# A second PSUM bank by turns for the products of the Fourier transforms

## The chip, the cores and the metric

The kernel runs on one core of a Trainium2 chip. The metric is the device time of one execution in microseconds (us). TensorE (PE, with its weight loads PEld) does the matmuls and writes PSUM; VectorE (DVE) and ScalarE (ACT) read PSUM; GpSimd (POOL) works on SBUF; SyncE (SP) issues most DMAs. All data are float32; a float32 matmul shows as two records on PE.

## The reference

```python
X = np.fft.rfft(x, axis=1)                    # x: 8 x 3008 x 256
Y = X * (filt_r + 1j * filt_i)[None, :, :]
y = np.fft.irfft(Y, n=3008, axis=1)
h = y.reshape(24064, 256) @ w_in              # 256 x 2048
g = h - np.tanh(h)
out = g @ w_out                               # 2048 x 256
```

## The kernel before

Two pieces of work lie side by side. The first is the filter in the frequency domain. A transform of 3008 points is done as 64 x 47, so each batch takes four steps of matmuls with constant matrices, with transposing trips through DRAM between them:

- `first`: 64-point transform, product `pf` (L351, L361), copied out by ACT (L352, L363).
- `middle`: 47-point transform, product `pz` (L430); then the filter: ACT writes a copy of `pz` with its halves exchanged to `zs` (L443, L444), DVE multiplies `pz` into `uv` (L445), POOL multiplies `zs` and adds it to `uv` (L446, L447). Then the inverse 47-point transform, product `pe` (L411), copied out by ACT (L414).
- `last`: inverse 64-point transform, product `pu` (L511), copied to `ut` by ACT (L513); POOL makes the sums `tu` of it (L524 to L527).

`middle` is a generator. Of its steps, one issues `pz` and what follows it, the next issues the `pe` of the step before. So `pz` and `pe` take turns, and a `pe` reads a `uv` that was begun one `pz` earlier. The second piece is the dense layer: up by `w_in` (`up`, L545), the nonlinearity (`shrink`, L611 to L621), down by `w_out` (`down`, L663). Both matrix products go by a scheme with seven block products in place of eight.

The batches are in five groups of one or two, `UNITS = [(0,), (1, 2), (3, 4), (5, 6), (7,)]`. While the dense layer of one of them runs, the transforms of the next are done in its gaps. The start ("prologue") does the transforms of batch 0 and has PSUM tiles of its own. Then a loop runs over 192 dense units `U`; four units make a quarter-by-quarter pass over the 2048 hidden columns for one chunk of rows. Unit `U` issues the `up` of `U`, the `shrink` of `U - 1` and the `down` of `U - 2`. The order on every engine is fixed by this program, since the schedule is manual.

Within `up`, `t(0)` to `t(4)` are the five places where one step of a transform is let in, at most one each. Here is the order around them on TensorE; `d()` issues matmuls of `down`:

```
X 1, Y 2, t(0), d, t(1), X 6, Z 5, d, t(2), X 7, d, t(3), X 4, d, t(4), Z 3
```

The numbers are the seven products. `X`, `Y` and `Z` are banks of PSUM. ACT copies `X` out after products 1, 6 and 7 (L551: `s1`, `u2`, `u3`), and DVE after product 4 (L590). DVE reads `Z` at L583 and L596. `Y` is written once, by product 2, and read once, by L569 on DVE. L569 is issued after `t(0)` and before `t(1)`. From there to the next unit's product 2 nothing uses `Y`.

A pool in which every tag has one buffer divides PSUM: `x`, `y`, `z`, four accumulators `o0` to `o3` of `down`, and `t`. Each is one of the eight banks. All products of the transforms in the loop are in `t`:

```python
psums.append(lambda name, shape: ps.tile(shape, F32, tag="t", bufs=1, name=name))
```

A new tile of a tag waits for the readers of the last tile of that tag. When steps of the transforms come is set by a list of positions (`steps`), and for `last` by the fourth unit of each chunk (slots 0 and 2). While batch 0's dense layer runs, in its units 8 to 21, nearly every slot has a product; later, for the pairs, less than half of the slots have one.

Of the kernel before, what the change touches and what calls it, by code (L numbers as in the profile page):

```python
# [9 lines left out]
F32 = mybir.dt.float32  # L10
# [38 lines left out]
def chunks_of(unit, size):  # L49
    n = steps_of(unit)  # L50
    return [(r, min(size, n - r)) for r in range(0, n, size)]
# [92 lines left out]
def kernel(  # L144
# [24 lines left out]
    def dram(t, off, dims):  # L169
        return bass.AP(tensor=t, offset=off, ap=[list(d) for d in dims])  # L170
# [136 lines left out]
    def weights_slow(tiles, quarters):  # L307

        jobs = parts_of(quarters)
        began = [begun(tiles, job, True) for job in jobs[:2]]  # L310
        yield
        for k in range(len(jobs)):
            for _ in began[k]:
                yield
            if k + 2 < len(jobs):
                began.append(begun(tiles, jobs[k + 2], True))
            if k % 2:
                sums(quarters[k // 2])
                yield
# [136 lines left out]
    def filter_rows(a, z):  # L456


        n, src = min(z, NK - 1) - a, (filt_r.tensor, filt_i.tensor)
        for row, m in ((0, LO), (LO, 16), (LO + 16, HI - 16)):  # L460
            low = row < LO
            at = a + 1 + NQ * row if low else NQ * (row - LO + 1) - 1 - a
            for v in range(2):
                yield v, row, m, 0, n, dram(src[v], at * DM,
                                            [[NQ * DM, m], [DM if low else -DM, n], [1, DM]])
        if z == NK:
            for v in range(2):
                yield v, v, LO - v, n, 1, dram(src[v], v * NQ * DM,
                                               [[NQ * DM, LO - v], [DM, 1], [1, DM]])
                yield v, LO, HI, n, 1, dram(src[v], NQ // 2 * DM,  # L470
                                            [[NQ * DM, HI], [DM, 1], [1, DM]])
# [282 lines left out]
    def store_some(n):  # L754
        for dst, src in outs[:n]:
            nc.sync.dma_start(dst, src)
        del outs[:n]
# [76 lines left out]
    psums = []  # L834
# [4 lines left out]
    with tc.tile_pool(name="tr", bufs=2) as tr, tc.manual_schedule():  # L839
        with tc.tile_pool(name="pro", bufs=1) as pro, \  # L840
# [136 lines left out]
            for j in range(NK // 2):  # L977
# [7 lines left out]
                for i in range(2):  # L985
                    k = (2 * j + i) % 4
# [34 lines left out]
        with tc.tile_pool(name="dn", bufs=2) as dn, \  # L1021
                tc.tile_pool(name="ps", bufs=1, space=bass.MemoryType.PSUM) as ps:

            psums.append(lambda name, shape: ps.tile(shape, F32, tag="t", bufs=1, name=name))

            y_sums = dn.tile([128, 2 * 4 * len(groups)], F32, bufs=1, name="y_sums")

            def psl(shape, tag):
                return ps.tile(shape, F32, tag=tag, bufs=1, name="pt")

            def tiles1(k, dtype, n):

                tag = {"raw": "ft", "it": "uv", "pt": "zs", "st": "e1", "ft": "a2"}[k]
                return tr.tile([128, n], dtype, tag=tag, bufs=2, name=k)

            def filters_d():
                zero = tr.tile([128, 4 * DM], F32, tag="a2", bufs=2, name="zero")
                G.memset(zero, 0.0)
                for p, bs in enumerate(UNITS[1:], 1):
                    nc.sync.dma_start(  # L1040
                        dram(ct1[p], NR * 64 * len(bs) * DM, [[DM, 64 * len(bs)], [1, DM]]),
                        zero[0:64 * len(bs), 0:DM])
                yield
                lo, hi = NR * 2 * NK * DM, IM * 2 * NK * DM
                while lo < hi:
                    n = min(128 * 4 * DM, hi - lo) // 128
                    nc.sync.dma_start(dram(filt_d, lo, [[n, 128], [1, n]]), zero[:, 0:n])
                    lo += 128 * n
                nc.sync.dma_start(dram(filt_d, (NK + NK - 1) * DM, [[DM, 1], [1, DM]]),
                                  zero[0:1, 0:DM])  # L1050
                yield
                for v, row, m, i, n, src in filter_rows(0, NK):
                    G.dma_start(dram(filt_d, ((row * 2 + v) * NK + i) * DM,
                                     [[2 * NK * DM, m], [DM, n], [1, DM]]), src)
                    yield

            late, copies = weights_slow(tiles1, range(7, 8)), filters_d()
            total = 4 * len(groups)
            for _ in last(0, z1):
                pass  # L1060
            next(late)
            for U in range(total + 2):
                i, u = divmod(U, 4)
                if U < total:
                    p, c = groups[i]
                    if c == 0 and u == 0:
                        units = 4 * len(CHUNKS[p])
                        steps, done = [], 0 if p else EARLY
                        if p + 1 < len(UNITS):
                            n_f = len(chunks_of(UNITS[p + 1], XH))  # L1070
                            n_m = 2 * NK // (3 - len(UNITS[p + 1]))
                            steps = [0.01 * units + 1.36 * units * (k - done) / (n_f - done)
                                     for k in range(n_f)]
                            lo, hi = 1.6 * units, 5 * units - 17
                            steps += [lo + (hi - lo) * k / n_m for k in range(n_m)]
                            ms = None
                    if u == 0 and i + 1 < len(groups) and c + 1 < len(CHUNKS[p]):
                        e2s[i + 1] = load_e2(*groups[i + 1])
                    if u == 2 and i + 1 < len(groups) and c + 1 == len(CHUNKS[p]):
                        assert done == len(steps)  # L1080
                        e2s[i + 1] = load_e2(*groups[i + 1])
                    if u == 0 and c + 1 == len(CHUNKS[p]) and p + 2 < len(UNITS):
                        fs = first(p + 2, z1)
                        next(fs)
                    if u == 2 and i + 1 < len(groups):
                        lasts = last(i + 1, z1)
                sh = shrink(U - 1) if 0 <= U - 1 < total else iter(())
                dw = down(U - 2) if 0 <= U - 2 < total else iter(())

                def d():  # L1090

                    next(dw, None)

                def e():

                    next(dw, None)

                def s():

                    next(sh, None)  # L1100

                def t(k):


                    nonlocal ms, done
                    if k == 2 and stores:
                        store(*stores.pop())
                    store_some(4)
                    if U >= total:
                        return  # L1110
                    pos = 20 * c + 5 * u + k
                    if u == 3 and k in (0, 2) and i + 1 < len(groups):
                        next(lasts)
                    elif done < len(steps) and steps[done] <= pos:
                        if done < n_f:
                            next(fs)
                        else:
                            next(ms)
                        done += 1
                        if done == n_f:  # L1120
                            ms = middle(p + 1, z1)
                            next(ms)
                    next(late, None)
                    if U > 0 and k in (1, 3):
                        next(copies, None)

                if U < total:
                    if U == total - 1:
                        one = tr.tile([128, 128], F32, tag="x", bufs=3, name="one_sb")
                        nc.sync.dma_start(one, one_d)  # L1130
                        ones = cst.tile([128, 1], F32, name="ones")
                        G.memset(ones, 1.0)
                    up(U, d, e, s, t)
                else:
                    for k in range(5):
                        s()
                        s()
                        d()
                        e()
                        t(k)  # L1140
                        if U == total + 1 and k == 0:
                            bounded(z1)
            for w in stores:
                store(*w)
            store_some(len(outs))
# [36 lines left out]
```

## Time and profile before

| | |
|---|---|
| time | 2831.02 us, median of 3 runs (2830.42 to 2831.22) |
| profiled span | 2831.1 us, granted TensorE clock 0.99 |
| busy, share of the span | PE 96%, PEld 80%, DVE 68%, ACT 66%, POOL 63% |
| chain that ended last | PE 78%, ACT 9%, issue 5%, DVE 5%, DMA 2% |

TensorE is busy in nearly every slice after the first two of forty. Ends of matmuls are modelled in the profile, so a short stall can hide within a busy time; starts are measured. A line of the timeline gives start, duration, engine, source line, operation, tiles, shapes and, in brackets, the idle time of the engine before it and what ended it. A line of the waits gives who waited for what: us in total, times, longest.

### The profile page before, as it was taken

Reading aid. Unit: us, or ns where it says so; the run is one execution under the profiler, and the core shown is the slowest. Engines: PE = TensorE matmul, PEld = TensorE weight load, DVE = VectorE, ACT = ScalarE, POOL = GpSimd, SP = SyncE. Lnnn points to the kernel's source line nnn. Section 1 sums busy time; section 2 is a strip of 40 time slices with the busy share of each in tenths; the row PEclk is TensorE's granted clock in tenths of the full one; section 3 lists DMA queues with packets and bytes.
Section 4 is the critical chain, followed back from the end, with each engine's and each line's share of the span. In section 5 each row is a group of like instructions: output and inputs, shape, how many; then the busy total and the mean of one; then the engine's idle time right before and its main releaser. Section 6 shows DMA issues by size and latency. Waiting matters only on the chain.

```text
span 2831.1 us, 36652 instructions
## 1 busy us (share of the span) xinstructions
PE 2730.9 (96%) x12438; PEld 2269.8 (80%) x12438; DVE 1911.7 (68%) x2175; ACT 1878.5 (66%) x2790; POOL 1792.0 (63%) x1407
## 2 busy tenths in 40 slices
PE   4899999999999999999999999999999999999998
PEld 2577777988878777888877887788888888898887
DVE  6755556666766677666666777676676767677776
ACT  2466666666666677666677666666666676667665
POOL 5546777544777767644576777755466667655555
PEclk7999999999999999999999999999999999999999
DMA  9854443233233322222333223212222322101010
GB/s 249 217 179 118 104 116 76 71 94 85 59 81 85 77 67 54 57 81 81 85 81 74 70 66 86 49 40 68 58 65 62 79 56 53 34 18 26 16 22 17
DMA packets 322592, 217.53 MB, mean 77 GB/s; under 512 B 224782, under 2 KB 274746, under 8 KB 322156
## 3 DMA queue, kind: packets, MB, share of 16 engines
q1 hardware_dynamic: 266826, 157.28, 23.6%
q10 hardware_dynamic: 52818, 51.53, 6.0%
q0 software_dynamic: 2752, 6.30, 0.8%
q8 instruction: 100, 1.64, 0.2%
q14 instruction: 96, 0.79, 0.1%
HBM read 138.87 MB, written 79.17 MB: 77 GB/s over the span
## 4 chain that ended last, share of the span: by engine, by line
PE 78%; ACT 9%; issue 5%; DVE 5%; DMA 2%; POOL 1%; ACTq 1%; SPq 0%; DVEq 0%; POOLq 0%
PE o L663 31%; PE x L545 20%; PE z L545 9%; PE y L545 6%; PE pe L411 3%; PE pu L511 3%; ACT y L611 3%; PE pz L430 3%; PE pf L351 2%; DVE h L617 1%; ACT u L551 1%; ACT zs L444 1%; DVE uv L445 1%; ACT y L612 1%; ACT zs L443 1%
## 5 line engine op out<-in xcount | busy, mean ns | idle before, releaser
L663 PE MATMUL o<-t,wd 128*128 128x256 f32 (+2 forms) x3072 | 776.3, 375 | 1.8 <-POOL t L526 1.3
L617 DVE TENSOR_TENSOR h<-h,y 128x1024 f32<-128x1024 f32 (+2 forms) x384 | 571.3, 1488 | 275.8 <-ACT y L612 275.8
L663 PEld LDWEIGHTS o<-t,wd 128*128 128x128 f32 x3072 | 580.7, 190 | 74.2 <-POOL t L526 1.6
L545 PE MATMUL x<-tu,wu 128*128 128x256 f32 (+2 forms) x2304 | 588.0, 377 | 9.2 <-ACT u L551 9.0
L663 PE MATMUL o<-h,wd 128*128 128x256 f32 (+2 forms) x2304 | 582.5, 375 | 0.4 <-DVE h L621 0.4
L621 DVE SCALAR_TENSOR_TENSOR h<-sq,h 128x1024 f32<-128x1024 f32 (+2 forms) x384 | 568.0, 1479 | 20.6 <-ACT y L611 0.5
L524 POOL TENSOR_TENSOR t<-h 128x512 f32<-128x512 f32 (+2 forms) x192 | 240.4, 1252 | 506.8 <-DVE h L621 455.0
L545 PEld LDWEIGHTS x<-tu,wu 128*128 128x128 f32 x2304 | 427.4, 190 | 151.8 <-issue 72.6
L663 PEld LDWEIGHTS o<-h,wd 128*128 128x128 f32 x2304 | 431.1, 190 | 71.8 <-issue 18.4
L618 ACT ACTIVATE sq<-y,near_b 128x1024 f32<-128x1024 f32 (+2 forms) x384 | 435.6, 1134 | 5.0 <-DVE h L621 0.2
L611 ACT ACTIVATE y<-h 128x1024 f32<-128x1024 f32 (+2 forms) x384 | 400.0, 1042 | 15.7 <-ACT e L414 8.0
L612 ACT ACTIVATE y<-y 128x1024 f32<-128x1024 f32 (+2 forms) x384 | 399.2, 1040 | 12.2
L551 ACT COPY s<-x 128x512 f32<-128x512 f32 (+2 forms) x192 | 110.8, 577 | 441.0 <-PE x L545 432.4
L527 POOL TENSOR_TENSOR t<-t,h 128x512 f32<-128x512 f32 (+2 forms) x192 | 308.9, 1609 | 0.1
L551 ACT COPY u<-x 128x512 f32<-128x512 f32 (+2 forms) x384 | 219.2, 571 | 56.9 <-PE x L545 22.2
L583 DVE TENSOR_TENSOR h<-z,u 128x512 f32<-128x512 f32 (+2 forms) x192 | 129.5, 675 | 180.0 <-ACT u L551 177.0
L525 POOL TENSOR_TENSOR t<-h,t 128x512 f32<-128x512 f32 (+2 forms) x192 | 240.9, 1255 | 15.1
L526 POOL TENSOR_TENSOR t<-h 128x512 f32<-128x512 f32 (+2 forms) x191 | 248.0, 1298 | 0.0
L446 POOL TENSOR_TENSOR zs<-zs,ft 128x512 f32<-128x512 f32 x112 | 165.4, 1477 | 101.8 <-ACT zs L444 101.6
L447 POOL TENSOR_TENSOR uv<-uv,zs 128x512 f32<-128x512 f32 x112 | 213.7, 1908 | 15.7 <-DVE uv L445 7.2
L545 PE MATMUL x<-ut,wu 128*128 128x256 f32 (+2 forms) x768 | 199.2, 382 | 6.9 <-DVE h L590 5.2
L569 DVE TENSOR_TENSOR h<-y,s 128x512 f32<-128x512 f32 (+2 forms) x192 | 130.4, 679 | 104.9 <-PE y L545 88.6
(122 smaller groups left out, 3380.2 us busy)
## 6 DMA issues: line engine op xcount, KB each, us to landing
a<-ct SPq DMA_DIRECT2D x64, 384.0 KB, 4.1
ft<-filt SPq DMA_DIRECT2D x96, 256.0 KB, 4.6
out_dram<-ot SPq DMA_DIRECT2D x1392, 16.0 KB, 1.5
ct<-e ACTq DMA_DIRECT2D x112, 192.0 KB, 2.4
ct<-a ACTq DMA_DIRECT2D x80, 256.0 KB, 2.9
x_sb<-in_x_dram SPq DMA_DIRECT2D x69, 256.0 KB, 2.8
e<-ct SPq DMA_DIRECT2D x33, 512.0 KB, 4.7
fg<-fg SPq DMA_DIRECT2D x40, 392.0 KB, 6.0
```

Source lines behind the costliest of these rows:

```text
L524: G.tensor_sub(t[0], b[0][1], b[0][0])
L525: G.tensor_sub(t[1], b[1][1], t[0])
L526: (V if shared else G).tensor_sub(t[2], b[1][1], b[0][1])
L527: G.tensor_sub(t[3], t[1], b[1][0])
L545: nc.tensor.matmul(bank[:, k], wu[:, q - 1, (2 * u + k) * 128:(2 * u + k + 1) * 128], rhs[q - 1], start=(first and k == 0), stop=True, ski ...
L551: ACT.copy(t, X)
L611: ACT.activation(y[k], ht[k], AF.Arctan, scale=S)
L612: ACT.activation(y[k], y[k], AF.Square, accum_out=y_sums[:, 2 * U + k // 2:2 * U + k // 2 + 1])
L617: V.tensor_mul(ht[k], ht[k], y[k])
L618: ACT.activation(sq[k], y[k], AF.Square, bias=near_b, scale=A)
L621: V.scalar_tensor_tensor(out=ht[k], in0=sq[k], scalar=K, in1=ht[k], op0=ALU.add, op1=ALU.mult)
L663: nc.tensor.matmul(product(q), wd[:, q - 1, (2 * u + k) * 128: (2 * u + k + 1) * 128], rhs[q - 1][:, k], start=(u == 0 and k == 0 and q == ...
```

## The change

The products of the transforms get a second bank, `Y`'s own, in those slots of a unit in which `Y` is free by the program's order: `t(1)`, `t(2)` and `t(3)`. There the tags go by turns: if the last product was in `t`, the next is in `y`, and otherwise in `t`. In `t(0)` and `t(4)` it is always `t`. The purpose is that a product need not wait until the one before it has been read.

```diff
-            psums.append(lambda name, shape: ps.tile(shape, F32, tag="t", bufs=1, name=name))
+            quarter, latest = [1], ["t"]
+
+            def zd(name, shape):
+                latest[0] = "y" if quarter[0] in (1, 2, 3) and latest[0] == "t" else "t"
+                return ps.tile(shape, F32, tag=latest[0], bufs=1, name=name)
+
+            psums.append(zd)
...
                     nonlocal ms, done
+                    quarter[0] = k
                     if k == 2 and stores:
```

The prologue keeps its own tiles. The two `pu` before the loop are at `quarter` 1: the first is in `y`, the second in `t`. In the unit with slots 0, 1, 2, 3, 4 all filled the banks are `t`, `y`, `t`, `y`, `t`. Of the 403 products from those two `pu` to the kernel's end, 164 are in `y`: 57 `pe`, 47 `pz`, 36 `pf`, 24 `pu`.

## The prediction

> **What bounds the kernel now.** I read the page first. TensorE is busy nearly always, and its idle time lies almost all in the start.
>
> ```profile
> PE 2730.9 (96%) x12438; PEld 2269.8 (80%) x12438; DVE 1911.7 (68%) x2175; ACT 1878.5 (66%) x2790; POOL 1792.0 (63%) x1407
> ```
>
> Busy time of matmuls is modelled, so I measured TensorE by the starts of its records instead. Equal records that follow each other start every 0.216 us (256 columns) or 0.433 us (512 columns). A stall is a start, less the start of the record before and that record's pace. From 150 us on, stalls sum to about 71 us, 2.5% of the span, and that bounds any gain there. Some 35 us of it stands before a product of the dense units into `x` (L545), spread thinly; 23 us before `pe` (L411), and these lie together: 22 us between 240 and 500 us. The windows show the same stage (start:end, then busy us of PE, PEld, DVE, ACT, POOL, then clock):
>
> ```profile
> 240.00:320.00 80.00, 73.41 (x295) 54.16 (x294) 45.13 (x51) 54.08 (x81) 64.44 (x46) 0.98 0.52 127
> ...
> 500.00:600.00 100.00, 100.00 (x472) 86.63 (x472) 63.50 (x74) 65.66 (x99) 46.45 (x40) 1.00 0.30 81
> ```
>
> In 240 to 320 us PE is short by 6.6 us of 80; at 500 us it is short by nothing. The first of these is where group 0's dense units (8 to 21) carry a transform product in nearly each of their five slots `t(0)` to `t(4)`; later stages fill less than half. The waits of TensorE, longest first, and one of DVE:
>
> ```profile
> PE pe L411 <- DVE uv L445: 15.3, 23, 2.7
> ```
> ```profile
> DVE uv L445 <- ACT zs L444: 124.5, 81, 5.2
> ```
>
> `pe` reads neither `pz` nor the `uv` just begun: its own `uv` is a step older. It waits for L445 because that is the last of three readers of `pz` (L443 and L444 on ACT, L445 on DVE), and `pz` holds the only bank, `t`. The timeline of unit 9 (start, us, engine, line; in brackets idle before it):
>
> ```profile
> 263.55 1.02 PE L430 MATMUL pz<-a,fg 94*128 94x512 f32 x2
> ...
> 266.58 0.59 ACT L443 ACTIVATE zs<-pz 64x512 f32<-64x512 f32 x1
> ...
> 267.18 0.58 ACT L444 COPY zs<-pz 64x512 f32<-64x512 f32 x1
> ...
> 267.44 0.59 PE L663 MATMUL o<-t,wd 128*128 128x256 f32 x2
> 267.61 1.23 DVE L621 SCALAR_TENSOR_TENSOR h<-sq,h 128x1024 f32<-128x1024 f32 x1
> ...
> 268.75 0.68 DVE L445 TENSOR_TENSOR uv<-pz,ft 128x512 f32<-128x512 f32 x1
> ...
> 269.58 1.07 PE L411 MATMUL pe<-uv,fg 112*96 112x512 f32 x2 [1.55 <-DVE uv L445]
> ...
> 273.08 1.02 PE L430 MATMUL pz<-a,fg 94*128 94x512 f32 x2
> ...
> 275.48 0.69 DVE L445 TENSOR_TENSOR uv<-pz,ft 128x512 f32<-128x512 f32 x1 [0.57 <-ACT zs L444]
> 276.08 0.68 DVE L590 COPY h<-x 128x512 f32<-128x512 f32 x1
> ...
> 276.31 1.07 PE L411 MATMUL pe<-uv,fg 112*96 112x512 f32 x2 [0.48 <-DVE uv L445]
> ...
> 278.09 1.03 PE L545 MATMUL x<-ut,wu 128*128 128x256 f32 x4
> ...
> 279.81 1.02 PE L430 MATMUL pz<-a,fg 94*128 94x512 f32 x2
> ...
> 282.20 0.69 DVE L445 TENSOR_TENSOR uv<-pz,ft 128x512 f32<-128x512 f32 x1 [3.23 <-ACT zs L444]
> ...
> 282.81 0.68 DVE L569 TENSOR_TENSOR h<-y,s 128x512 f32<-128x512 f32 x1
> ...
> 283.04 1.07 PE L411 MATMUL pe<-uv,fg 112*96 112x512 f32 x2 [0.48 <-DVE uv L445]
> ```
>
> Look at the first `pe`: TensorE was free at 267.44 + 2 x 0.216 = 267.87 and began at 269.58, 0.146 us after L445's end: 1.71 us lost. The last five of these lines are unit 10's start: there DVE does L445 first and L569, the reader of `Y`, after it.
>
> **What the Trainium skill says.** "Perfetto Trace Analysis", section "Matmuls": independent groups of matmuls should rotate through different PSUM banks, so that the evacuation of one lies beside the next one's matmuls. That is what the change is, and the waits above agree that the evacuation is exposed. "PSUM — Partial Sum Buffer", section "PSUM bank collisions raise a hardware error": two engines may not touch one bank and quadrant at once, reads against reads included, so they have to be serialised by bank. The trace agrees: L445 starts only when L444 is done (267.18 + 0.58, then L621, then 268.75; 274.81 + 0.58 to 275.48). Same page, "Engine vs sequencer instructions": ScalarE and VectorE queues are strictly first in, first out. So a reader of `Y` can be late because of what stands ahead of it.
>
> **The change part by part.** No instruction is added, removed or moved: the order on every engine is that of before. Only the bank of 164 of the 403 products changes from `t` to `y`, and with it which readers a matmul waits for. A product in `y` waits for L569 of its unit, or for the readers of the last product in `y`. A product in `t` waits for the readers of the last one in `t`, now two products back or more. `Y`'s own matmuls of the next unit wait for the last product there. I put the new bank of each product beside the old trace's ends of readers, with the measured 0.146 us from a reader's end to the matmul:
>
> 1. Units 9, 13, 17, slot 2: `pe` in `t` after `pz` in `y`. 1.72 + 1.70 + 1.72 = 5.14 us of stall end; `t` was last read by L414 at 262.6 us in unit 9, long before.
> 2. Slot 4 of units 9, 11, 13, 15, 17, 19: `pe` in `t`, `pz` of slot 3 in `y`. 6 x 0.64 = 3.85 us end.
> 3. Slot 3 of the even units 10 to 20: `pe` in `y`. 0.43 + 0.48 + 0.43 + 0.52 + 0.43 + 0.75 = 3.03 us end.
> 4. Slot 1 of those even units: `pe` goes into `y` with `pz` of slot 0 in `t`. It now waits for L569, which stands on DVE behind L445. In unit 10 TensorE is free at 282.40; L569 ends at 283.49, so it begins at 283.64: 1.24 in place of 0.64. Queued behind this `pe` on TensorE are `x` of product 6 and all that follows. Six units: 3.52 us added.
> 5. Unit 21, slot 2: 2.83 us end. Unit 8, slot 1: 3.03 becomes 3.12, since L569 and the older `uv` hold it there too: 0.09 added.
>
> That makes 5.14 + 3.85 + 3.03 + 2.83 - 3.52 - 0.09 = 11.2 us.
>
> 6. What takes over. In unit 9 TensorE would come 1.71 + 0.64 = 2.36 us sooner to the next unit's first `x`, which waits for L590 (reads `x`). Margin now: 278.09 - 276.76 - 0.146 = 1.18. L590 follows L445, which can move up by only the 0.57 us that DVE idles before it. So 1.18 + 0.57 = 1.75 us get through and 0.6 are lost, in units 9, 13 and 17: 1.8 us given back. In units 11, 15, 19 the 0.64 us fit within a margin of 1.17.
> 7. `pu` at slot 2 of the last unit of a group: `pu` of slot 0 is in `t`, that of slot 2 mostly in `y`, or in `t` after a product in `y`. Five stalls, 1.7 us in all. I count half, 0.8, as an ACT chain hangs on `pu` as well. Two later `pe` lose 0.09 us each.
> 8. The start: the second `pu` waits 2.63 us at 122.2 us and a `pf` 1.08 at 141.9. I count nothing. The next `x` wait there for the sums on GpSimd (L524 cannot begin before 124.6, its queue is full of L260 to L263) and for ACT's copy L551, which stands behind other ACT work; so these hide it.
> 9. `Y`'s matmuls: from the last reader of a product in `y` to them, the least distance over 192 units is 1.47 us. No wait. Outside the dense stage L569 is done at least 0.16 us, mostly 0.6 to 1.5 us, before a slot-1 product wants `y`. No wait.
>
> Sum: 11.2 - 1.8 + 0.8 - 0.2 = 10.0 us; 2831.0 - 10.0 = 2821.0 us.
>
> **The rivals.**
> - Given back on `x`. ACT and DVE in the dense stage hold chains through the one bank `x`; POOL is busy 64.4 of 80 us. If all that units 9, 13, 17 gain comes back there, 5.14 + 1.92 us go, and 11.2 - 7.1 = 4.1 us are left: 2827. For it: the margin of 1.2 us. Against: ACT idles 1.2 us before L443 and L551 in the even units, so the lag is made up.
> - More. If nothing is given back, `pu` counts in full and the start brings its 3.7 us: 11.2 + 1.7 + 3.7 = 16.6, so 2814.5. Against: step 8.
> - Slower: a wait for `Y` in place of one for `t`. 60 products stand in `y` at slot 1 behind L569, 46 outside the units 8 to 21. If in half of these (23) one more DVE operation (1.48 us, L617 or L621) fell ahead of L569, each would wait 1.48 - 0.59 = 0.89: 20 us lost against 10 won, 2841. Against: DVE's order is unchanged, and the trace has not one such case there now.
>
> **How the numbers follow.** Forecast 0.65, given back 0.17, more 0.10, slower 0.08. Time: 2821. Faster by over 0.2% is below 2825.4: 0.75. Within: 0.17. Slower: 0.08. The range takes in the case of more to within half a us, and that of given back with 2 us for the sizes: 2815 to 2829.
>
> **What would show it.** Right: `pe` behind L445 falls from 15.3 us to near nothing, with a new wait of `pe` behind L569 (some 7 us modelled idle or less); PE in 240 to 320 us rises from 73.4 by some 3; from 500 us on all runs the same, some 10 us earlier; the first `x` of a unit waits for L590 a little in units 10, 14, 18. Step 6 is wrong if waits of `x` grow by over 4 us, step 8 if the start up to 150 us moves by over 1 us, step 9 if `y` shows waits on TensorE. The forecast as a whole is wrong if PE in 240 to 320 us stays below 75.

## The result and the profile after

The changed kernel takes 2817.9 us (median of 6 runs, 2814.6 to 2821.0) where the kernel before takes 2831.1. The ratio is 0.9951, with a 95% interval of 0.9939 to 0.9964. So 13.2 us are won (10.2 to 17.3 by the interval); 10.0 were forecast.

The page of the changed kernel, its first lines: as many matmul records as before (12438), in less time.

```profile
span 2817.1 us, 36653 instructions
...
PE 2725.6 (97%) x12438; PEld 2268.1 (81%) x12438; DVE 1913.8 (68%) x2175; ACT 1877.0 (67%) x2790; POOL 1796.2 (64%) x1407
```

The windows of the same two stages (start:end, then busy us of PE, PEld, DVE, ACT, POOL, then clock):

```profile
240.00:320.00 80.00, 74.85 (x305) 56.34 (x304) 48.52 (x52) 56.71 (x85) 66.00 (x46) 0.98 0.53 129
...
500.00:600.00 100.00, 100.00 (x454) 84.22 (x453) 66.20 (x74) 66.26 (x99) 48.14 (x39) 1.00 0.29 82
```

TensorE does ten matmul records more in the 80 us from 240 on than before (305 against 295). Its waits between 150 and 2700 us, all of them:

```profile
PE x L545 <- ACT u L551: 8.5, 24, 0.7
PE pe L411 <- DVE h L569: 4.2, 4, 1.1
PE pe L411 <- POOL uv L447: 3.7, 2, 2.9
PE x L545 <- DVE h L590: 3.0, 7, 0.5
PE pe L411 <- POOL t L526: 2.2, 2, 1.1
PE pf L361 <- ACT a L363: 1.2, 1, 1.2
PE pe L411 <- DVE uv L445: 0.7, 2, 0.3
```

The wait of `pe` behind L445 was 15.3 us and is 0.7. A new one stands behind L569: six times 1.1 us. Two of the six are put down to L526 on POOL, which ended at about the same moment. The timeline of unit 9 and of the start of unit 10:

```profile
267.14 1.02 PE L411 MATMUL pe<-uv,fg 112*96 112x512 f32 x2
...
268.01 0.68 DVE L445 TENSOR_TENSOR uv<-pz,ft 128x512 f32<-128x512 f32 x1
...
273.38 1.02 PE L411 MATMUL pe<-uv,fg 112*96 112x512 f32 x2
...
274.06 0.68 DVE L445 TENSOR_TENSOR uv<-pz,ft 128x512 f32<-128x512 f32 x1
274.24 1.03 PE L545 MATMUL z<-ut,wu 128*128 128x256 f32 x4
...
274.65 0.68 DVE L590 COPY h<-x 128x512 f32<-128x512 f32 x1
...
275.39 1.13 PE L545 MATMUL x<-ut,wu 128*128 128x256 f32 x4
```
```profile
279.61 0.69 DVE L445 TENSOR_TENSOR uv<-pz,ft 128x512 f32<-128x512 f32 x1 [1.88 <-ACT zs L444]
280.22 0.68 DVE L569 TENSOR_TENSOR h<-y,s 128x512 f32<-128x512 f32 x1
...
281.05 1.07 PE L411 MATMUL pe<-uv,fg 112*96 112x512 f32 x2 [1.08 <-DVE h L569]
```

In unit 9 `pe` at 267.14 starts while `pz` has still not been read: L445 ends 1.55 us later. Before the change, `pe` had to come after L445. Before the `pe` of slot 4 (273.38) there is no idle time either: L445 ends at 274.74, 1.4 us after its start. Then the first `x` of unit 10 should follow `z` after 4 x 0.216 = 0.86 us, at 275.10; it starts at 275.39, 0.06 us after L590's end. That is the wait of step 6. The last `pe` waits for L569, which is second to L445 on DVE: step 4.

The start of each unit's `Y` (the first matmul of product 2) gives a ruler that does not depend on modelled ends. From one such start to the next is a unit's length. In us (differences and forecasts are for all units of a row together):

| unit | before | changed | difference | forecast |
|---|---|---|---|---|
| 8 | 21.19 | 21.19 | 0.00 | +0.09 |
| 9, 13, 17 | 18.85, 18.84, 18.85 | 16.99, 17.00, 16.99 | -5.57 | -7.06 + 1.8 given back |
| 10, 14, 18 | 17.56, 17.56, 17.56 | 17.68, 17.68, 17.68 | +0.36 | +0.51 |
| 11, 15, 19 | 17.14, 17.15, 17.71 | 16.46, 16.46, 17.02 | -2.06 | -1.93 |
| 12, 16 | 17.61, 17.66 | 17.68, 17.68 | +0.09 | +0.19 |
| 20 | 17.14 | 16.87 | -0.27 | -0.22 |
| 21 | 19.49 | 16.00 | -3.49 | -2.83 |
| 9 to 21 together | 233.10 | 222.17 | -10.93 | -9.5 |
| 22 to 190 together | 2300.50 | 2298.27 | -2.23 | -0.6 |

The 2.23 us come from five units, 47, 59, 95, 107 and 151. These are the units of the five stalls of `pu` of step 7; they are shorter by 0.60, 0.23, 0.59, 0.23 and 0.58 us. The other stretches between them move by up to 0.3 us either way, which cancels. Together 10.93 + 2.23 = 13.2 us, as much as the medians differ by. The two profiled spans differ by 14.0; most of the rest, 0.7 us, lies before unit 1's `Y`, where profiles of equal code repeat less well (step 8 below).

### The profile page after: what moved, and what is told of

It reads as the page before. It is cut to its first block, busy times and chain, and to the rows that moved or that the text cites. A ratio compares the mean times of both kernels' runs of the same rounds, so it can differ in the third digit from the quotient of the medians.

```text
span 2817.1 us, 36653 instructions
## 1 busy us (share of the span) xinstructions
PE 2725.6 (97%) x12438; PEld 2268.1 (81%) x12438; DVE 1913.8 (68%) x2175; ACT 1877.0 (67%) x2790; POOL 1796.2 (64%) x1407
## 4 chain that ended last, share of the span: by engine, by line
PE 79%; ACT 8%; DVE 4%; issue 4%; DMA 3%; POOL 2%; ACTq 0%; SPq 0%; DVEq 0%; POOLq 0%
PE o L663 32%; PE x L545 20%; PE z L545 9%; PE y L545 5%; PE pe L411 3%; PE pu L511 3%; PE pz L430 3%; ACT y L611 2%; PE pf L351 2%; ACT u L551 1%; DVE h L617 1%; ACT zs L444 1%; ACT zs L443 1%; ACT y L612 1%; DVE h L590 1%
## 5 line engine op out<-in xcount | busy, mean ns | idle before, releaser
L551 ACT COPY s<-x 128x512 f32<-128x512 f32 (+2 forms) x192 | 110.7, 577 | 441.6 <-PE x L545 433.0
L551 ACT COPY u<-x 128x512 f32<-128x512 f32 (+2 forms) x384 | 218.9, 570 | 56.8 <-PE x L545 20.3
L526 POOL TENSOR_TENSOR t<-h 128x512 f32<-128x512 f32 (+2 forms) x191 | 248.0, 1298 | 0.0
L446 POOL TENSOR_TENSOR zs<-zs,ft 128x512 f32<-128x512 f32 x112 | 168.6, 1505 | 91.8 <-ACT zs L444 91.7
L447 POOL TENSOR_TENSOR uv<-uv,zs 128x512 f32<-128x512 f32 x112 | 210.7, 1881 | 15.6 <-DVE uv L445 7.2
L569 DVE TENSOR_TENSOR h<-y,s 128x512 f32<-128x512 f32 (+2 forms) x192 | 130.3, 679 | 102.0 <-PE y L545 89.1
```

Source lines behind the costliest of these rows:

```text
L526: (V if shared else G).tensor_sub(t[2], b[1][1], b[0][1])
L551: ACT.copy(t, X)
```

## The experiments

Times are medians, beside the kernel before on the same chip. The lengths of stretches are from the ruler above; between profiles of equal code nearly every unit from 9 on repeats to some hundredths of a us, and the sums to 0.13.

### Only in units 8 to 21, and only outside them

```diff
-                    quarter[0] = k
+                    quarter[0] = k if 8 <= U <= 21 else 0      # e1, first quarter 0 too
+                    quarter[0] = 0 if 8 <= U <= 21 else k      # e2
```

> The turns between the two banks are kept in the dense units 8 to 21 alone; all other products are in t. My theory (the gain is the stalls of pe behind the readers of pz in this stage): unit 22's Y comes about 10.9 us earlier than in the kernel before, as in the changed kernel between units 9 and 22, and from there to the end nothing more is won: 2820 us, span 11 us shorter. Rival (the gain comes mostly from the start, from pu and from the waits of x spread over the rest): under 5 us are left, 2826 or more.

> The complement: units 8 to 21 use t alone, all others take turns. My theory: the stalls of pe in units 9 to 21 come back in full, and what is left is 0.7 us of the start and some 2 us of pu at slot 2 of a group's last unit: 2828 us, span about 3 us shorter than before. Rival: 8 us or more are won, 2823 or less.

With the turns in units 8 to 21 alone the kernel takes 2823.0 us, ratio 0.9974 (0.9963 to 0.9984). Units 9 to 21 take 222.17 us, to the hundredth what they take in the changed kernel, and units 22 to 190 take 2300.57, as before. The median is 3 us above what was expected. In its profile 1.2 us of them lie ahead of unit 8, where the program is that of before: unit 8's `Y` comes at 240.06 us, in the kernel before at 238.91. With the turns everywhere else it takes 2828.7 us, ratio 0.9993 (0.9985 to 1.0002). Units 9 to 21 take 233.03 and units 22 to 190 take 2298.05. Its wait of `pe` in the stage between 239 and 494 us is the one of before:

```profile
PE pe L411 <- DVE uv L445: 14.6, 21, 2.7
```

By the ruler the two parts add up, and five sixths of the gain come from 14 of 192 units. By the medians they give 7.5 and 1.8 us, 9.2 of the 13.2. Where the other 4 us went in these runs is not shown.

### The read of Y ahead of slot 0

```diff
         s1 = copied("s1")
+        V.tensor_add(h[:, 0, :, 0:w], Y, s1)
         t(0)
         d()
         shrinks(0)
-        V.tensor_add(h[:, 0, :, 0:w], Y, s1)
```

> The changed kernel with DVE's read of Y (the sum h<-y,s) issued ahead of slot 0, so that it stands before the reading of pz into uv on DVE. My theory (pe at slot 1 of the even units 10 to 20 waits 1.24 us only because of this order on DVE): these six stalls and their 7.2 us go, ACT's copy u2 has a margin of 1.65 us there and takes nothing back: about 2811 us, each even unit 1.1 to 1.2 us shorter. Rival (in these units ACT works without a gap from zs to u2, so TensorE only waits for u2 a little later): under 2 us are won, 2816 or more.

2813.5 us, ratio 0.9945 (0.9931 to 0.9959). Units 9 to 21 take 217.61 us, 4.56 less than in the changed kernel. The even units are shorter by 0.51 (10, 14, 18), 1.13 (12, 16) and 0.85 (20), not by 1.2 each. It was measured again beside the changed kernel on one chip:

> The changed kernel again, beside the next run on the same chip. Theory: 2818 us; unit by unit the same as in its first profile but for the start and for half-clock stretches, each worth 1.7 us, which come or stay away after the 3 us stall at 245 us.

> The kernel with Y read ahead of slot 0 again. Theory: 4.6 us less than the changed kernel from the six even units (their slot-1 stalls fall from 1.24 us to the 0 to 0.7 us that GpSimd's uv leaves), so about 2813 us. Rival (the first measurement was the half clock at 245 us that happened to stay away, 1.7 us): 2816 or more.

2816.6 us against 2812.5, ratios to before 0.9949 (0.9936 to 0.9963) and 0.9930 (0.9916 to 0.9943). Units 9 to 21: 222.17 against 217.50. For TensorE between 239 and 477 us in this kernel the view of the waits lists one line:

```profile
PE pe L411 <- POOL uv L447: 5.9, 7, 2.9
```

L569 is gone from it (its line is L566 here), so the order on DVE was the cause of the 1.24 us. What came in its place is GpSimd: `pe` now waits for its own `uv`, in seven places where it was two. In units 10, 14 and 18 that is 0.67 to 0.70 us by starts in place of 1.24. That is most of why 4.6 us were won and not 7.2. GpSimd was busy 66.0 of 80 us already in the changed kernel's window above.

```diff
         # the kernel before, one bank t, with the same move
+        V.tensor_add(h[:, 0, :, 0:w], Y, s1)
         t(0)
```

> The kernel before, with one bank t for all products, and DVE's read of Y issued ahead of slot 0 as in e3_y_read_first. My theory (that order matters only where a product waits for Y): nothing changes in units 9 to 21 by over 0.3 us in all, 2831 us. Rival (the order by itself frees DVE or x, and e3's gain over the changed kernel has nothing to do with the second bank): 4 to 7 us are won, 2825.

2831.9 us, ratio 1.000 (0.9991 to 1.0008). Units 9 to 21 take 233.04 against 233.10. The move alone is worth nothing; it pays only where a product wants `Y`.

### Slot 4 too

```diff
-                latest[0] = "y" if quarter[0] in (1, 2, 3) and latest[0] == "t" else "t"
+                latest[0] = "y" if quarter[0] in (1, 2, 3, 4) and latest[0] == "t" else "t"
```

> The turns are taken in slot 4 as well, one product before the next unit's Y. By the ends of the readers in the old trace, 26 products are in y at slot 4 and six of the following Y matmuls (pz in y) would wait 0.6 to 1.0 us, 4.1 us in all, against 1.2 us that two pe at slot 4 no longer wait. My theory: 3 us slower than the changed kernel, 2821 us, and waits of y behind uv (L445) on TensorE. Rival (a wait for Y costs nothing since x's own wait stands there anyway): equal to the changed kernel.

2820.7 us, ratio 0.9966 (0.9952 to 0.9980). Units 22 to 190 take 2301.24 us against 2298.27 in the changed kernel: 2.97 more, as worked out. (The intervals of the ratios of the two kernels, 0.9952 to 0.9980 and 0.9939 to 0.9964, overlap; the ruler tells them apart.) From 494 us on a wait stands in its profile that the changed kernel does not have:

```profile
PE y L545 <- DVE uv L445: 2.6, 6, 0.7
```

So in this kernel the last slot in which `Y` is free at no cost is slot 3. Units 9 to 21 are the same in both kernels: where all five slots are full, slot 4 stays in `t` by the turns.

### Unit 21 alone

```diff
-                    quarter[0] = k
+                    quarter[0] = k if U == 21 else 0
```

> The turns are taken in dense unit 21 alone, the rest is the kernel before. There a stall of 2.83 us before pe at slot 2 ended in a stretch of 3.41 us at half the granted TensorE clock. My theory (the stall costs 2.83 us and the half clock that follows it 0.5 x 3.41 = 1.7 us more; pe at slot 3 then waits 1.0 us for its own uv from GpSimd): no half-clock stretch near 484 us, and units 21 to 22 are 3.5 us shorter than in the kernel before. Rival (the clock there has nothing to do with this stall): the stretch stays, and 1.8 us are won.

One run, 2829.7 us. Unit 21 is 3.68 us shorter than before, and no other of the units 9 to 30 changes by over 0.02 (3.49 us were won in this unit by the changed kernel). The windows of the kernel before show why it is more than the stall (the number behind the POOL count is the granted clock):

```profile
484.58:487.99 3.41, 3.41 (x9) 2.52 (x8) 0.20 (x1) 1.35 (x3) 0.82 (x1) 0.50 0.20 55
487.99:494.00 6.01, 6.01 (x30) 5.21 (x29) 4.76 (x8) 1.89 (x4) 1.92 (x3) 1.00 0.13 37
```

After the stall of 2.83 us TensorE ran 3.41 us at half its clock. With the turns in unit 21 alone the clock is whole there:

```profile
484.00:486.00 2.00, 1.46 (x7) 0.95 (x5) 1.05 (x4) 1.60 (x6) 1.22 (x1) 1.00 0.07 21
486.00:488.00 2.00, 1.90 (x7) 1.38 (x8) 1.97 (x4) 1.40 (x2) 0.09 (x2) 1.00 0.28 77
```

So 2.83 us of stall and 0.5 x 3.41 = 1.7 us of slow clock go; the new wait for `uv` at slot 3 takes 0.9 back here (1.1 in the changed kernel). That the slow clock comes from this stall does not rest on one run: the three profiles that have the stall (before, the turns only outside units 8 to 21, `Y` read first with one bank) have the stretch after it, and the nine others have neither.

### The copy of x ahead of the reading of pz

```diff
+            def rest(uv=uv, zs=zs, pz=pz, fr=fr, fi=fi):     # in middle: L445 to L447
...
+            if hold[0]: held.append(rest)
+            else: rest()
...
+        hold[0] = U in (9, 11, 13, 15, 17, 19)
         t(3)
+        hold[0] = False
         mm(X, 4, False)
         V.tensor_copy(h[:, 2, :, 0:w], X)
+        while held: held.pop()()
```

The edit is shortened here. GpSimd's two operations on `uv` (L446, L447) are put off together with L445.

> The changed kernel, with DVE's copy of x (product 4 into h) put ahead of the reading of pz from slot 3, in units 9, 11, 13, 15, 17 and 19. My theory (in units 9, 13 and 17 part of the won time is given back because the next unit's first x waits for this copy, which stands behind that reading): the 0.3 us before that x goes in each, units 9, 13 and 17 are 0.2 to 0.3 us shorter than in the changed kernel, 11, 15 and 19 the same; 0.9 us in all. Rival (ACT's chain of copies of x gives it back, whatever DVE's order): no unit changes by over 0.1 us.

One run, 2817.1 us. So short a gain does not show in one time, but it does by the ruler. Units 9, 13 and 17 are 0.40, 0.40 and 0.39 us shorter than in the changed kernel; all others from 9 to 21 are the same to 0.01. In its timeline (where the lines of `up` are L553) the first `x` of unit 10 follows `z` after 0.86 us, with no wait:

```profile
273.49 1.03 PE L553 MATMUL z<-ut,wu 128*128 128x256 f32 x4
274.35 1.03 PE L553 MATMUL x<-ut,wu 128*128 128x256 f32 x4
```

Both reorderings together:

> Both reorderings on DVE together: the read of Y ahead of slot 0, and the copy of x ahead of the reading of pz from slot 3 in units 9 to 19. My theory (they remove two different waits, slot 1 of the even units and the first x after units 9, 13 and 17): the sum of what each won less what they share, 0.4 us for the first of these units and less for the others, so 0.5 to 1.2 us below the kernel with Y read first: about 2812 us. Rival (what the first leaves is bound by GpSimd's uv, which then takes the second gain too): the same as with Y read first, 2813 us.

2812.1 us, ratio 0.9929 (0.9915 to 0.9942). Here the theory missed: beside the kernel with `Y` read first, unit 9 is 0.41 us shorter and unit 10 is 0.38 longer, units 13 and 17 gain nothing, and units 9 to 21 are the same to 0.04 us. All waits of TensorE that the view lists from 237 to 475 us are for GpSimd:

```profile
PE pe L413 <- POOL uv L450: 6.3, 7, 2.9
```

So in this stage no wait in the view is for DVE any more; those that stand are for GpSimd. What holds GpSimd up was not tested. Of all versions that ran, the one with `Y` read first and this one are the fastest, and they can't be told apart.

## Why the prediction was right, point by point

The time (2817.9 in a range of 2815 to 2829), the direction and the place were right. By its steps:

- Steps 1 to 3: stalls of 5.14 + 3.85 + 3.03 us end. They ended: `pe` behind L445 fell from 15.3 us to 0.7. Units 11, 15 and 19, which have only step 2's term, gained 0.69 each where 0.64 was given. That they belong to these units was shown by the two kernels that split the turns.
- Step 4: 0.64 us becomes 1.24 at slot 1 of the even units. By starts it is 1.24 us in units 10, 12, 14, 16 and 18 and 1.17 in unit 20. That L569's place behind L445 is the cause was shown by the kernel with `Y` read first.
- Step 5: Unit 8 was given 0.09 us and took none. Unit 21 was mis-sized. It gave 3.49 us and not 2.83, because two terms were left out: the slow clock after the stall (1.7 us) and a new wait for `uv` at slot 3 (1.1 us). That the two partly cancel is luck. The sign of the first was there in the trace before: after the stall at 484 us the records start further apart than elsewhere.
- Step 6: 1.8 us given back in units 9, 13 and 17. The wait for L590 was right; its size was 1.2 us (three times 0.40, shown by the copy of `x` put first). Another 0.2 us in each of these units stand before the `x` of product 7, behind ACT's copy of product 6 (L551), which the step did not have. A gain of 1.86 us in unit 9 got through where 1.75 was worked out.
- Step 7: `pu`. Counted at half, 0.8 us; it gave 2.23. The stalls themselves are 1.69 us, and each held the record behind it up by another 0.11. No chain on ACT took any of it back. This is the largest miss of a term.
- Step 8: nothing from the start. The second `pu` stalls for 2.1 to 2.6 us by starts in the four profiles without turns there. In all eight with turns that stall is gone, and about as much stands before the first `x` and a `pf` instead (1.63 and 1.10 us in the changed kernel). So that the next work hides it was right. What the step left out is the clock again: in three of the four a stretch at half clock follows the stall, and in none of the eight. From the first `pu` to unit 1's `Y` these three took 16.51 to 17.06 us, the fourth 15.48, and the eight 14.76 to 16.06. So the start gives something only in a run in which the slow stretch falls away.
- Step 9: no wait for `Y`. None is in the profile, and the experiment with slot 4 shows that the distance worked out from ends of readers tells where one would come.

The sum: 9.4 us were forecast for units 8 to 21 (11.2 less 1.8) and 10.93 came; 0.6 for the rest (0.8 less 0.2) and 2.2 came. So the forecast was 3 us short, half of that on `pu`. The rival "given back on `x`" held for the waits of step 6 and no more: over the whole stretch from 150 to 2700 us TensorE's waits before `x` are 11.5 us by the view both before and after. The rival "more" had the right answer on `pu` and the wrong one on the start.

One of the forecast's own tests failed. PE busy in 240 to 320 us was to rise by some 3 and not to stay below 75; it is 74.85. The test was badly made, not the steps. Summed for this window the steps give less: stalls of 1.71 + 0.64 + 0.43 + 0.64 us end in units 9 to 11, 0.60 + 0.60 + 0.09 are added in units 10, 12 and 8, and 0.6 is given back in unit 9. That makes 1.5 us and not 3; 1.4 came. The window also lies at fixed times while the work moves, and modelled ends hide some 0.16 us of each stall (the first `pe` of unit 9 waited 1.71 us by starts and 1.55 by the view). Units, not windows, should have been compared.

## What to carry to other kernels

When a matmul waits for the last reader of a buffer that it does not itself need, look for a bank that is idle by program order at that point; it may belong to quite another part of the kernel. What decides is then who reads that bank, and what stands ahead of that reader in its engine's queue: put the reader first and the bank is free sooner. The Trainium skill's "Perfetto Trace Analysis", section "Matmuls", gives the general rule on rotating banks; here a second bank was worth 13.2 us, and the order of one VectorE instruction a further 4.6 us that was worth nothing without it.

## What the runs showed of the hardware that was not expected

A stall of TensorE can cost more than its length. The stall before `pe` in unit 8 is the same, by starts, in all twelve profiles (3.03 to 3.04 us). In six of them 3.41 us at half the clock follow it, and unit 8 takes 21.2 us; in the other six none follow, and it takes 19.5. Here are two profiles of the same kernel, the changed one, in windows at the same time:

```profile
245.58:249.00 3.42, 3.42 (x9) 2.66 (x8) 2.22 (x2) 2.02 (x3) 3.34 (x2) 0.50 1.04 248
```
```profile
245.58:249.00 3.42, 3.42 (x15) 2.64 (x14) 2.85 (x2) 2.09 (x3) 3.34 (x2) 1.00 1.05 245
```

Nine matmul records in one, fifteen in the other. The Trainium skill's "TensorE: Matmul & The Clock Gate", section "What's actually happening", says that the clock is set by activity in windows of 3413 ns that run freely, not in step with the program. The traces agree: within each profile the half-clock stretches start whole multiples of 3.413 us apart. In the kernel before, those at 122.77, 245.65 and 484.58 us are 36 and 70 such steps apart. So each profile has its own grid of windows, and the same stall falls differently into it.

The same section has the clock fall after at least one idle window of some 3.4 us. Here less was enough. Between 115 and 2780 us the twelve profiles have twelve half-clock stretches, and each starts at the end of a window of which one stall had filled 0.61 or more, that is 2.1 us. Of the other stalls of 1 us and more one filled as much (0.62) without a stretch after it; the rest filled at most 0.57. So the same stall of 3.03 us costs 1.7 us more or nothing more, by how it falls into the windows. Such a stretch is part of why runs of one kernel differ by some us here: of the 2.4 us between the profiled spans of the changed kernel (2817.1 and 2814.7) it makes 1.7.
